# Moving the gate product to the middle of a pair, and casting k before summing it

## The chip, the cores and the metric

The kernel runs on one core of a Trainium2 chip. The core has a matrix engine (TensorE, "PE" in the profile, with its weight loads as "PEld"), VectorE (DVE), ScalarE (ACT), GpSimd (POOL) and SyncE (SP), which issues most DMAs. Each engine works through its own instruction queue; they meet at semaphores. The metric is the device time of one execution in microseconds (us). The runs of the kernel before took 334.65, 334.62 and 332.92 us.

## The reference

A block-sparse causal attention (4 batches, 8 heads, 768 positions, head size 64) is followed by a Fourier mix and a feed-forward layer. The part of the attention around the change, shortened:

```python
k_rep = k.reshape(B, H, 12, 64, D).mean(axis=3)          # one mean per block of 64 keys
gate_scores = np.einsum('bhsd,bhnd->bhsn', q, k_rep)
gate_scores = np.where(causal, gate_scores, -1e9)
top_idx = np.argsort(gate_scores, axis=-1)[..., -3:]     # the three best blocks, and the own block
scores = np.matmul(q, k.transpose(0, 1, 3, 2)) / np.sqrt(D)
scores = np.where(mask_of(top_idx, own_block) & (pos[:, None] >= pos[None, :]), scores, -1e9)
attn = softmax(scores)
attn_out = np.matmul(attn, v)
...
X = np.real(np.fft.fft(np.fft.fft(x, axis=1), axis=2))    # x: attn_out as (4, 768, 512)
u = x + X
un = (u - mean(u)) / np.sqrt(var(u) + 1e-6)
out = u + np.maximum(un @ w_ch1, 0.0) @ w_ch2             # 512 -> 2048 -> 512
```

## The kernel before

Two heads of a batch make a pair, and there are 16 pairs (`kk` from 0 to 15, four to a batch). Each pair goes through these stages, which are functions in the code:

- `stage_AA(kk, who)` calls `stage_A` for two halves. With `who=1` it transposes k: three matmuls (L279) put half of the positions into a PSUM tile `tp`. From this tile VectorE sums k over blocks (`kr12`, L292), and the tile is also cast to 16 bits into `kI` in two pieces, one for each head `e` (L311 on ScalarE; below pair 7 one of the four pieces of a pair is cast by VectorE, L309). After the second half the sums are copied into the operand of the gate product (`kr24`, L297; from pair 8 on split into two 16-bit parts `krx`, L304 and L305). With `who=0` it transposes q, copies it from PSUM (L285, from pair 8 on L287 and L288), and GpSimd copies it on into `qg` (L240).
- `stage_B` is the gate product: ten fp32 matmuls with q and the block sums (L323; ten 16-bit ones from pair 8 on, L331). VectorE adds the causal term (`gsb`, L325), finds the eight largest values ten times (`mx`, L340) and writes the mask `gmp` (L342, L346 or L348).
- `stage_C` transposes the mask on PE (`gt`, L354), and VectorE copies it into rows 64 to 75 of `qg` for either head (L357). The scores then contain the mask, since `kI` holds large negative numbers in the same rows.
- `stage_S` is one sixth of the scores: step `p` of a pair is third `p % 3` of head `p // 3`. Matmuls (L386, and L390 for the diagonal below pair 7) fill one of two PSUM tiles `sc`, and ScalarE's exponential (L391) empties it into `ptl`. So a step's matmuls wait for the exponential two steps earlier.
- `stage_AV(kk, e)` multiplies by v (21 matmuls, L412); VectorE normalises (`rcp` L417, `x` L418). Head 1 of a pair also runs `fold`, additions for the Fourier step, mostly on GpSimd.

All PSUM tiles but `sc` share a pool of four buffers. PE and GpSimd run in the order in which the code emits their work (`tc.manual_schedule`). For VectorE, ScalarE and the DMA queues a scheduler chooses the order, work that is emitted earlier having priority when it is ready.

The main loop (L729 to L766) emits, for each pair, six steps. Every step emits `stage_S`, then some filler, then the other stages that a table assigns to the step, then filler again. Before the change the steps of a usual pair `kk` hold: step 0 the k transposes of pair `kk + 2` (A1); step 1 the output of pair `kk - 1`, head 1 (AV1); step 2 the q transposes of pair `kk + 2` (A0), the v cast on GpSimd, and the issue of the q and k loads of pair `kk + 4` on SP; step 3 the gate transposes of pair `kk + 1` (C); step 4 the output of this pair's head 0 (AV0); step 5 the gate product of pair `kk + 2` (B). The v loads of pair `kk + 2` are issued in step 0. Pair 6 (`NORM_SLOT`) has another table, since the normalisation of batch 0 falls into it; its missing gate product, that of pair 8, runs in step 1 of pair 7. A prologue prepares pairs 0 and 1 up to their gate products, with `stage_W` matmuls on constants in between.

Filler is the Fourier mix and the feed-forward work: `stage_S1` and `stage_S2` (Fourier, L480 to L521), `stage_N` (normalisation), `stage_T` (transposes, L562), `stage_M1` (L578) and `stage_M2` (L592). `filler` pulls as much as a running credit allows, counted by half steps. Units of the chain S1, S2, T become due by a planned clock `feed.now`, to which every emitted stage adds a planned cost and which advances by at least `PACE` for each step; gaps such as `s1_gap` keep a unit from being emitted before its inputs can be there.

Of the kernel before, what the change touches and what calls it, by code (L numbers as in the profile page):

```python
# [118 lines left out]
def kernel(  # L119
# [9 lines left out]
    nc = tc.nc  # L129
    B, H, S, D = q.shape  # L130
# [133 lines left out]
    def stage_A(kk, who, g):  # L264
        d = P[kk]
        src = d["qn"] if who == 0 else d["kn"]
        if who == 0 and g == 0:
            d["qt"] = apool.tile([128, S], FP, tag="qT32", name=f"qT32_{kk}")
            if kk >= SPLIT:
                parts = d["qt"].bitcast(F16)  # L270
                d["qh"], d["ql"] = parts[:, 0:S], parts[:, S:2 * S]
            d["qg"] = [qg_t[e][kk % 3] for e in range(2)]
        if who == 1 and g == 0:
            d["kI"] = [kI_t[e][kk % 3] for e in range(2)]
            d["kr12"] = spool.tile([128, NB], FP, tag="kr12", name=f"kr12_{kk}", bufs=2)
            d["kr24"] = kr24_t[kk % 2]
        ps = pst([128, 3, 128], f"tp_{kk}_{who}_{g}")
        for i in range(3):
            nc.tensor.transpose(ps[:, i, :],  # L279
                                src[:, 3 * g + i, :, :].rearrange("p h d -> p (h d)"), id32)  # L280
        flat = ps.rearrange("p a c -> p (a c)")
        cols = slice(384 * g, 384 * (g + 1))
        if who == 0:
            if kk < SPLIT:
                (nc.scalar.copy if kk == LATE else nc.vector.tensor_copy)(out=d["qt"][:, cols], in_=flat)  # L285
            else:
                nc.scalar.activation(out=d["qh"][:, cols], in_=flat, func=AF.Copy, scale=QS)  # L287
                STT(out=d["ql"][:, cols], in0=flat, scalar=QS, in1=d["qh"][:, cols], op0=MULT, op1=SUB)  # L288
            if g == 1 and kk != LATE:
                cast_q(kk)  # L290
        else:
            nc.vector.tensor_reduce(out=d["kr12"][:, 6 * g:6 * g + 6],  # L292
                                    in_=ps.rearrange("p a (x c) -> p a x c", x=2),
                                    axis=mybir.AxisListType.X, op=ADD)
            if g == 1 and kk < SPLIT:
                for e in range(2):
                    nc.vector.tensor_copy(out=d["kr24"][64 * e:64 * e + 64, NB * e:NB * (e + 1)],  # L297
                                          in_=d["kr12"][64 * e:64 * e + 64, :])
            elif g == 1:
                d["krx"] = krx_t[kk % 2]  # L300
                for e in range(2):
                    r, c = slice(64 * e, 64 * e + 64), slice(NB * e, NB * (e + 1))
                    hi, lo = d["krx"][r, 0, c], d["krx"][r, 1, c]
                    nc.vector.tensor_scalar(out=hi, in0=d["kr12"][r, :], scalar1=QS, scalar2=None, op0=MULT)  # L304
                    STT(out=lo, in0=d["kr12"][r, :], scalar=QS, in1=hi, op0=MULT, op1=SUB)  # L305
            for e in range(2):
                dst, src_ = d["kI"][e][0:64, cols], flat[64 * e:64 * e + 64]
                if kk < EARLY and g == 1 and e == 1:
                    nc.vector.tensor_copy(out=dst, in_=src_)  # L309
                else:  # L310
                    nc.scalar.copy(out=dst, in_=src_)  # L311


    NG = NST - 1
# [287 lines left out]
    def queue_batch(b, start):  # L602
        last = start
        units = []

        s1_gap = 6.0 if b else 3.5
        s2_gap = 1.8 if 0 < b < B - 1 else 1.0
        t_gap = {0: 4.0, B - 1: 6.0}.get(b, 7.5)
        for dt in (1, 0):
            last = Unit(lambda dt=dt: stage_S1(b, dt), S1_COST, last, s1_gap if dt == 1 else 0.0)  # L610
            units.append(last)
        for kt in range(NST):
            last = Unit(lambda kt=kt: stage_S2(b, kt), S2_COST, last, 2.5 if kt == 0 else s2_gap)
            units.append(last)
        for st in range(NST):
            last = Unit(lambda st=st: stage_T(b, st), T_COST, last, t_gap if st == 0 else 0.2,
                        allowed=(lambda: b == 0 or m1_left[b - 1] == 0))
            units.append(last)

        def arm():  # L620
            def m1(it):
                stage_M1(b, it)
                m1_left[b] -= 1
            for it in range(NIT):
                feed.bulk.append(Unit(lambda it=it: m1(it), M1_COST))
# [11 lines left out]
    def filler(kk, half):  # L637


        i = 12 * kk + half  # L640
        key = 12 * (3 * NP) + 32
        if i < key:
            work, left = 2 * BATCH + 3 * CHAIN, key - i
        else:
            work, left = 2 * BATCH + 3 * CHAIN + (NIT - 4) * M1_COST, 12 * NK - i
        state["credit"] = min(state["credit"], 1.0) + (work - state["spent"] - state["credit"]) / left
        done = feed.pull(state["credit"])
        state["credit"] -= done
        state["spent"] += done

    def main(fn, cost, *a):
        fn(*a)
        feed.spend(cost)
# [2 lines left out]
        stage_A(kk, who, 0)  # L656
        stage_A(kk, who, 1)

    PACE = 1.4
    with tc.manual_schedule(engines={mybir.EngineType.PE, mybir.EngineType.Pool}):  # L660
        nc.vector.memset(warm, 0.0)
        nc.scalar.dma_start(id32, dr["ident32"].ap())
# [46 lines left out]
        def after_av(kk):  # L709
            b, hp = divmod(kk, NP)  # L710
            if hp == NP - 1:
                u = Unit(lambda: None, 0.0)
                u.done(feed.now)
                queue_batch(b, u)

        @contextmanager
        def behind_norm(kk):

            if kk != NORM_SLOT:
                yield  # L720
                return
            with tc.issue_after(X[0]["normed"].ins):
                yield

        USUAL = dict(A1=0, AV1=1, A0=2, C=3, AV0=4, B=5)
        NORM = dict(A1=4, AV1=1, A0=5, C=3, AV0=4, B=6)
        for kk in range(NK):  # L729
            at = NORM if kk == NORM_SLOT else USUAL  # L730
            for p in range(6):
                t_in = feed.now
                main(stage_S, 0.39, kk, p // 3, p % 3)
                filler(kk, 2 * p)
                if p == 0 and kk + 2 < NK:
                    load_v(kk + 2)
                if p == at["AV1"] and kk > 0:
                    with behind_norm(kk):
                        main(stage_AV, 0.65, kk - 1, 1)
                    after_av(kk - 1)  # L740
                if p == 1 and kk - 1 == NORM_SLOT:
                    main(stage_B, 0.35, kk + 1)
                if p == at["A1"] and kk + 2 < NK:
                    main(stage_AA, 0.7, kk + 2, 1)
                if p == at["C"] and kk + 1 < NK:
                    main(stage_C, 0.3, kk + 1)
                if p == at["AV0"]:
                    main(stage_AV, 0.65, kk, 0)
                    if kk + 2 == LATE:
                        pool_after(ft[3][:, 0, 2:3])  # L750
                        cast_q(kk + 2)
                        cast_v(kk + 2)
                if p == at["A0"]:
                    if kk + 2 < NK:
                        main(stage_AA, 0.7, kk + 2, 0)
                        if kk + 2 != LATE:
                            cast_v(kk + 2)
                    if kk == 0:
                        stage_W(4)
                    if kk + 4 < NK:  # L760
                        load_qk(kk + 4)
                if p == at["B"] and kk + 2 < NK:
                    main(stage_B, 1.05 if kk + 2 < SPLIT else 0.35, kk + 2)
                filler(kk, 2 * p + 1)
                if feed.now < t_in + PACE:
                    feed.now = t_in + PACE  # L766
            if kk == 1:
                load_fft()
            if kk in (2, 4):
                pool_after(P[kk + 2]["qt"])  # L770
                load_w1(kk // 2 - 1)
            if kk in (6, 7):
                pool_after(P[kk + 2]["qt" if kk + 2 < SPLIT else "ql"])
                load_w2(2 * kk - 12)
                load_w2(2 * kk - 11)
# [35 lines left out]
```

## Time and profile before

| what | us |
|---|---|
| runs: median (lowest to highest) | 334.62 (332.92 to 334.65) |
| profiled execution, device time | 332.94 |
| its span, first to last instruction | 331.2 |
| first score matmul of pairs 0, 1, 2, 3, 4, 5, 6 | 16.66, 24.85, 32.88, 40.84, 48.73, 62.22, 73.43 |
| first feed-forward matmul (L578) | 86.95 |
| last exponential of the attention starts | 249.3 |

A row of a timeline gives start, length, engine, line, operation, tiles and count; a bracket at its end says how long the engine sat idle before it, and what ended that. Equal instructions in a row are merged into one line. In the chain of waits the lengths are those by which the end was held up, not the durations. The busy time of PE includes the pipeline's latency: matmuls of 512 columns overlap and follow each other at 0.216 us where nothing stops them (96 in 20.73 us near the end), while the row of their group says 379 ns for one.

Between pair 0 and the first feed-forward matmul there is little filler, and a pair takes about 8 us. Later a step carries about 2 us of filler, and a pair takes 18 to 20 us.

### The profile page before, as it was taken

The numbers are of one execution on the slowest core, as the hardware profiler recorded it, in microseconds if no ns is written. First come the engines' busy times: TensorE is split into PE (matmuls) and PEld (weight loads), VectorE is DVE, ScalarE is ACT, GpSimd is POOL, SyncE is SP. The second block draws the span as 40 slices with busy tenths as digits, with TensorE's granted clock in tenths as the row PEclk, the third lists the DMA queues.
The fourth block names the chain that finished last, engine by engine and source line by source line (L and its number), as shares of the span: only waits on it lengthen the run. The fifth ranks groups of instructions, "written<-read, shape, count | busy, mean of one in ns | idle before, by whom it ended". The sixth has DMA issues, their size and how long they took to land.

```text
span 331.2 us, 7008 instructions
## 1 busy us (share of the span) xinstructions
PE 311.9 (94%) x2712; PEld 202.9 (61%) x2712; DVE 235.7 (71%) x750; ACT 180.3 (54%) x276; POOL 84.7 (26%) x137
## 2 busy tenths in 40 slices
PE   8799998997889989998999989999999999999995
PEld 3567776876656666555666666656666654556442
DVE  3778889689776898999765898998457588433211
ACT  3188889789965855428486754535764302244000
POOL 8545573352481120504032030502030000000000
PEclk9999999998999999999999999999999999999999
DMA  8997999990799242425324000010000011100021
GB/s 203 230 256 186 246 136 226 155 221 7 165 188 181 54 96 75 103 70 136 99 48 97 2 0 35 32 65 32 34 2 0 2 64 63 65 1 2 32 95 63
DMA packets 85312, 31.18 MB, mean 94 GB/s; under 512 B 77736, under 2 KB 81136, under 8 KB 85280
## 3 DMA queue, kind: packets, MB, share of 16 engines
q1 hardware_dynamic: 79984, 25.88, 31.4%
q0 software_dynamic: 3552, 4.40, 8.5%
q10 hardware_dynamic: 1744, 0.46, 0.6%
q8 instruction: 21, 0.34, 0.4%
q14 instruction: 11, 0.09, 0.1%
HBM read 28.63 MB, written 6.29 MB: 105 GB/s over the span
## 4 chain that ended last, share of the span: by engine, by line
PE 73%; DVE 16%; ACT 7%; issue 1%; POOL 1%; DVEq 0%; ACTq 0%
PE ch L592 22%; PE ha L578 14%; PE sc L386 8%; PE hb L578 7%; PE av L412 5%; ACT kI L311 4%; PE g L323 3%; PE za L480 2%; DVE mx L340 2%; DVE ptl L397 2%; ACT ptl L391 2%; PE tp L279 2%; PE warm L365 2%; PE gt L354 2%; PE mx L507 2%; PE mx L508 2%
## 5 line engine op out<-in xcount | busy, mean ns | idle before, releaser
L391 ACT ACTIVATE ptl<-sc 128x896 f16<-128x896 f32 x96 | 87.3, 919 | 45.9 <-PE sc L386 36.6
L592 PE MATMUL ch<-w_sb,hT 128*128 128x512 f16 x384 | 91.4, 379 | 0.5 <-DVE qT L288 0.5
L578 PEld LDWEIGHTS <-w_sb 128*128 128x128 f16 x512 | 48.8, 97 | 38.6 <-issue 4.7
L578 PE MATMUL ha<-unT,w_sb 128*128 128x512 f16 x256 | 65.7, 378 | 1.8 <-DVE hT L583 1.4
L386 PE MATMUL sc<-qg,kI 76*128 76x512 f16 (+3 forms) x256 | 54.8, 306 | 3.6 <-ACT ptl L391 3.6
L592 PEld LDWEIGHTS <-hT 128*128 128x128 f16 x384 | 36.2, 97 | 35.1 <-issue 0.6
L581 ACT ACTIVATE hT<-ha 128x512 f16<-128x512 f32 x64 | 38.1, 597 | 33.5 <-PE ha L578 33.4
L583 DVE TENSOR_SCALAR hT<-hb 128x256 f16<-128x256 f32 x64 | 26.8, 421 | 28.9 <-PE hb L578 28.7
L578 PE MATMUL hb<-unT,w_sb 128*128 128x256 f16 x256 | 38.4, 272 | 1.1 <-ACT hT L581 0.7
L429 POOL TENSOR_TENSOR fs<-x 128x384 f16<-128x384 f16 x12 | 10.9, 909 | 105.5 <-DVE x L418 91.8
L386 PEld LDWEIGHTS <-kI 76*128 76x128 f16 x256 | 24.0, 100 | 20.3 <-issue 2.8
L311 ACT CAST kI<-tp 64x384 f16<-64x384 f32 x57 | 27.1, 475 | 14.6 <-DVE kr L292 13.6
L595 DVE TENSOR_TENSOR u<-ch,u 128x512 f32<-128x512 f32 x24 | 16.5, 685 | 19.9 <-PE ch L592 19.6
L412 PE MATMUL av<-v,ptl 128*128 128x65 f16 x672 | 26.2, 195 | 0.0
L412 PEld LDWEIGHTS <-ptl 128*128 128x128 f16 x672 | 24.8, 98 | 2.0
L292 DVE TENSOR_REDUCE kr<-tp 128x6 f32<-128x384 f32 x32 | 17.2, 551 | 7.0 <-PE tp L279 7.0
L397 DVE TENSOR_TENSOR ptl<-ptl,ut 128x384 f16<-128x384 f16 x36 | 16.0, 479 | 6.1 <-ACT ptl L391 5.7
L553 ACT ACTIVATE x<-u,nmr,rstd 128x512 f16<-128x512 f32 x12 | 8.9, 806 | 17.7 <-DVE nmr L546 17.6
L418 DVE TENSOR_TENSOR x<-av,rcp 128x384 f16<-128x384 f32 x32 | 17.8, 557 | 0.9
L390 PE MATMUL sc<-ltri,id 128*128 128x128 f16 x84 | 18.4, 219 | 0.0
L240 POOL COPY qg<-qT 64x768 f16<-64x768 f16 x16 | 14.4, 902 | 12.1 <-ACT qT L287 11.6
L520 DVE BATCH_NORM_STATS2 bst<-u 128x6 f32<-128x512 f32 x24 | 16.6, 692 | 1.2 <-ACT u L516 0.7
(112 smaller groups left out, 422.9 us busy)
## 6 DMA issues: line engine op xcount, KB each, us to landing
vn<-in_v_dram SPq DMA_DIRECT2D x32, 192.0 KB, 3.3
out_dram<-u SPq DMA_DIRECT2D x24, 256.0 KB, 2.0
kn<-in_k_dram SPq DMA_DIRECT2D x30, 192.0 KB, 3.3
qn<-in_q_dram SPq DMA_DIRECT2D x30, 192.0 KB, 3.4
w_sb<-in_moe_w_ch_dram POOLq DMA_DIRECT2D x8, 256.0 KB, 7.0
w_sb<-in_moe_w_ch_dram POOLq DMA_DIRECT2D x4, 512.0 KB, 9.5
cs_sb<-c_CS SPq DMA_DIRECT2D x1, 289.5 KB, 4.9
ss_sb<-c_SS SPq DMA_DIRECT2D x1, 289.5 KB, 5.2
```

The costliest lines, as they stand in the source:

```text
L292: nc.vector.tensor_reduce(out=d["kr12"][:, 6 * g:6 * g + 6], in_=ps.rearrange("p a (x c) -> p a x c", x=2), axis=mybir.AxisListType.X, op=ADD)
L311: nc.scalar.copy(out=dst, in_=src_)
L386: nc.tensor.matmul(sp[:, co:co + (a1 - a0)], d["kI"][e][0:76, 128 * jt:128 * (jt + 1)], d["qg"][e][0:76, a0:a1], start=True, stop=not diag)
L390: nc.tensor.matmul(sp[:, co:co + 128], id16, ltri, start=False, stop=True)
L391: nc.scalar.activation(out=pt[:, SEC * s:SEC * (s + 1)], in_=sp[:, 0:SEC], func=AF.Exp, scale=0.125 if kk < SPLIT else 0.125 / QS)
L397: nc.vector.tensor_tensor(out=dg, in0=dg, in1=um, op=MULT)
L412: nc.tensor.matmul(av[:, st, 0:65], pt[:, o:o + 128], d["v16"][:, e, jt, 0:65], start=(cnt == 0), stop=(cnt == 20))
L418: nc.vector.tensor_tensor(out=x_b[:, :, 64 * h:64 * h + 64], in0=av[:, :, 0:64], in1=rcp.to_broadcast([128, NST, 64]), op=MULT)
L578: nc.tensor.matmul(hp_, w1_sb[:, dt, 128 * it:128 * (it + 1)], unT[:, dt, c0:c1], start=(dt == 0), stop=(dt == NDT - 1))
L581: nc.scalar.activation(out=hT[:, c0:c1], in_=hp_, func=AF.Relu)
L583: nc.vector.tensor_scalar(out=hT[:, c0:c1], in0=hp_, scalar1=0.0, scalar2=None, op0=mybir.AluOpType.max)
L592: nc.tensor.matmul(cps, x["hT"][it][:, 128 * st:128 * (st + 1)], w2_sb[:, it, :], start=(it == 0), stop=(it == NIT - 1))
```

## The change

Three things change, and the amount of work is the same before and after.

First, k. From pair 2 on a half of k is cast before it is summed, and the casts and the sum of the second half are not emitted with its transposes, but by `finish_k`, after the scores of the next step. So they stand behind that step's exponential.

Second, the table of steps. A usual pair `kk` now has in step 0 A1 of pair `kk + 2`; in step 1 B of pair `kk + 1`; in step 2 AV1 of pair `kk - 1`; in step 3 A0 of pair `kk + 2`, with its casts and loads, and C of pair `kk + 1`; in step 4 AV0; in step 5 nothing. A gate product thus runs in the pair directly before the one that uses it, two steps ahead of its transposes. Pair 0 has no gate product. Pair 4 keeps AV1 in step 1, has B in step 2, A0 in step 3 and C ahead of AV0 in step 4. Pair 5 has a second gate product, that of pair 7, in step 5.

Third, the planner: `PACE` goes from 1.4 to 1.3, and some gaps of the chain become shorter.

```diff
-            nc.vector.tensor_reduce(out=d["kr12"][:, 6 * g:6 * g + 6],
-                                    in_=ps.rearrange("p a (x c) -> p a x c", x=2),
-                                    axis=mybir.AxisListType.X, op=ADD)
...
+            if kk < 2:
+                sums_k(kk, g, ps)
+                cast_k(kk, g, ps)
+            elif g == 0:
+                cast_k(kk, g, ps)
+                sums_k(kk, g, ps)
+            else:
+                d["tp_k"] = ps
+
+    def finish_k(kk):
+
+        ps = P[kk].pop("tp_k", None)
+        if ps is not None:
+            cast_k(kk, 1, ps)
+            sums_k(kk, 1, ps)
+
+    def cast_k(kk, g, ps):
+        d = P[kk]
+        flat = ps.rearrange("p a c -> p (a c)")
+        cols = slice(384 * g, 384 * (g + 1))
+        for e in range(2):
+            dst, src_ = d["kI"][e][0:64, cols], flat[64 * e:64 * e + 64]
+            if kk < EARLY and g == 1 and e == 1:
+                nc.vector.tensor_copy(out=dst, in_=src_)
+            else:
+                nc.scalar.copy(out=dst, in_=src_)
+
+    def sums_k(kk, g, ps):
...
-        s1_gap = 6.0 if b else 3.5
-        s2_gap = 1.8 if 0 < b < B - 1 else 1.0
-        t_gap = {0: 4.0, B - 1: 6.0}.get(b, 7.5)
+        s1_gap = 6.0 if b else 3.2
+        s2_gap = 1.8 if 0 < b < B - 1 else 1.0 if b else 0.8
+        t_gap = {0: 3.4, B - 1: 6.0}.get(b, 7.0)
...
-            last = Unit(lambda kt=kt: stage_S2(b, kt), S2_COST, last, 2.5 if kt == 0 else s2_gap)
+            last = Unit(lambda kt=kt: stage_S2(b, kt), S2_COST, last, (2.5 if b else 2.2) if kt == 0 else s2_gap)
...
-    PACE = 1.4
+    PACE = 1.3
...
-        USUAL = dict(A1=0, AV1=1, A0=2, C=3, AV0=4, B=5)
-        NORM = dict(A1=4, AV1=1, A0=5, C=3, AV0=4, B=6)
+        USUAL = ["A1", "B", "AV1", "A0 C", "AV0", ""]
+        LAYOUT = {
+            0: ["A1", "", "", "A0 W C", "AV0", ""],
+
+            NP: ["A1", "AV1", "B", "A0", "C AV0", ""],
+            NORM_SLOT - 1: ["A1", "B", "AV1", "A0 C", "AV0", "B+"],
+
+            NORM_SLOT: ["", "AV1", "", "C", "A1 AV0", "A0"],
+        }
         for kk in range(NK):
-            at = NORM if kk == NORM_SLOT else USUAL
             for p in range(6):
                 t_in = feed.now
                 main(stage_S, 0.39, kk, p // 3, p % 3)
+                if kk + 2 < NK:
+                    finish_k(kk + 2)
                 filler(kk, 2 * p)
                 if p == 0 and kk + 2 < NK:
                     load_v(kk + 2)
...
+                for what in LAYOUT.get(kk, USUAL)[p].split():
...
+                    n = kk + (2 if what == "B+" else 1)
+                    if what in ("B", "B+") and n < NK:
+                        main(stage_B, 1.05 if n < SPLIT else 0.35, n)
                 filler(kk, 2 * p + 1)
```

`sums_k` holds the sum and the copies or splits that follow it, as they stood in `stage_A` before (L292 to L305).

More of the change, by code (lines that the diff above doesn't have):

```diff
@@ L291, in stage_A @@
         else:
-            nc.vector.tensor_reduce(out=d["kr12"][:, 6 * g:6 * g + 6],
-                                    in_=ps.rearrange("p a (x c) -> p a x c", x=2),
-                                    axis=mybir.AxisListType.X, op=ADD)
[L295 to L305, printed above, removed]
@@ L306, in stage_A @@
-            for e in range(2):
[L307 to L311, printed above, removed]
+            if kk < 2:
[6 more added lines that the diff above has]
+                d["tp_k"] = ps
@@ new lines, in sums_k @@
+    def sums_k(kk, g, ps):
+        d = P[kk]
+        nc.vector.tensor_reduce(out=d["kr12"][:, 6 * g:6 * g + 6],
+                                in_=ps.rearrange("p a (x c) -> p a x c", x=2),
+                                axis=mybir.AxisListType.X, op=ADD)
+        if g == 1 and kk < SPLIT:
+            for e in range(2):
+                nc.vector.tensor_copy(out=d["kr24"][64 * e:64 * e + 64, NB * e:NB * (e + 1)],
+                                      in_=d["kr12"][64 * e:64 * e + 64, :])
+        elif g == 1:
+            d["krx"] = krx_t[kk % 2]
+            for e in range(2):
+                r, c = slice(64 * e, 64 * e + 64), slice(NB * e, NB * (e + 1))
+                hi, lo = d["krx"][r, 0, c], d["krx"][r, 1, c]
+                nc.vector.tensor_scalar(out=hi, in0=d["kr12"][r, :], scalar1=QS, scalar2=None, op0=MULT)
+                STT(out=lo, in0=d["kr12"][r, :], scalar=QS, in1=hi, op0=MULT, op1=SUB)
@@ L736 @@
                     load_v(kk + 2)
[L737 to L754, printed above, removed]
+                for what in LAYOUT.get(kk, USUAL)[p].split():
+                    if what == "AV1" and kk > 0:
+                        with behind_norm(kk):
+                            main(stage_AV, 0.65, kk - 1, 1)
+                        after_av(kk - 1)
+                    if what == "AV0":
+                        main(stage_AV, 0.65, kk, 0)
+                        if kk + 2 == LATE:
+                            pool_after(ft[3][:, 0, 2:3])
+                            cast_q(kk + 2)
+                            cast_v(kk + 2)
+                    if what == "A1" and kk + 2 < NK:
+                        main(stage_AA, 0.7, kk + 2, 1)
+                    if what == "A0" and kk + 2 < NK:
                         main(stage_AA, 0.7, kk + 2, 0)
@@ L757 @@
                             cast_v(kk + 2)
-                    if kk == 0:
+                        if kk + 4 < NK:
+                            load_qk(kk + 4)
+                    if what == "W":
                         stage_W(4)
[L760 to L763, printed above, removed]
+                    if what == "C" and kk + 1 < NK:
+                        main(stage_C, 0.3, kk + 1)
+                    n = kk + (2 if what == "B+" else 1)
+                    if what in ("B", "B+") and n < NK:
+                        main(stage_B, 1.05 if n < SPLIT else 0.35, n)
                 filler(kk, 2 * p + 1)
```

## The prediction

> **What bounds the kernel now.** I began with busy shares, then cut the span into attention pairs, then followed the chain of waits through one pair, and last read what one engine does in it. All sums are made against the profiled execution: 332.94 us, of which 331.2 us are span.
>
> ```profile
> PE 311.9 (94%) x2712; PEld 202.9 (61%) x2712; DVE 235.7 (71%) x750; ACT 180.3 (54%) x276; POOL 84.7 (26%) x137
> ```
>
> ```profile
> 24.85:32.88 8.03, 7.34 (x99) 6.01 (x99) 6.65 (x26) 6.71 (x10) 4.16 (x5) 1.00 0.75 181
> 32.88:40.84 7.96, 7.34 (x99) 6.01 (x99) 6.65 (x26) 6.71 (x10) 4.12 (x6) 1.00 1.05 256
> ```
>
> The first block is the page's shares, the second a table by stretch (columns: length, then busy PE, PEld, DVE, ACT, POOL, then clock, DMA, GB/s). I cut at the first score matmul of pairs 1, 2 and 3; pair 0 begins at 16.66. PE's 94% is an average over two stages. From 87 us to the end PE carries the feed-forward work and its waits, summed, are only 5.1 us up to 285 us; nothing that the change does to attention can win more than that there. Before 87 us no engine is full: a pair takes 8 us while PE, ACT and DVE are each busy for 6.7 to 7.3. A loop of waits sets that pace:
>
> ```profile
> 31.96 1.10 PE g L323 x10
> ...
> 33.40 0.82 DVE mx L340 x10
> 34.22 0.47 DVE kr L292
> ...
> 34.71 0.47 ACT kI L311
> ...
> 36.17 0.82 ACT ptl L391
> ...
> 37.13 0.38 PE sc L386
> ```
>
> The chain of waits (start, length, what): the gate product ends, VectorE takes its maxima, then sums k, then ScalarE casts k three times (34.71 to 36.17), then comes an exponential, and only then has the next score matmul a free buffer. A cast begins 0.02 us after the sum that it follows: the two readers of one transposed tile take turns. Now the same stretch on VectorE:
>
> ```profile
> 33.08 0.28 DVE L325 TENSOR_TENSOR gsb<-g,cz 128x120 f32<-128x120 f32 x1 [0.80 <-PE g L323]
> 33.40 0.82 DVE L340 MAX8 mx<-gsb 128x8 f32<-128x12 f32 x10
> 34.13 0.55 DVE L292 TENSOR_REDUCE kr<-tp 128x6 f32<-128x384 f32 x1
> 34.59 0.28 DVE L342 TENSOR_TENSOR gmp<-gsb,mx 128x120 f16<-128x120 f32 x1
> 34.77 0.56 DVE L292 TENSOR_REDUCE kr<-tp 128x6 f32<-128x384 f32 x1
> 35.24 0.22 DVE L346 TENSOR_TENSOR gmp<-gmp,oth 128x120 f16<-128x120 f16 x1
> 35.37 0.35 DVE L297 COPY kr<-kr 64x12 f32<-64x12 f32 x2
> 35.75 0.20 DVE L417 RECIPROCAL rcp<-av 128x6 f32<-128x6 f32 x1
> ...
> 36.57 0.56 DVE L309 CAST kI<-tp 64x384 f16<-64x384 f32 x1
> 37.16 1.02 DVE L285 COPY qT<-tp 128x384 f32<-128x384 f32 x2
> 38.21 1.00 DVE L357 COPY qg<-gt 12x640 f16<-12x640 f16 x2
> 39.46 0.20 DVE L417 RECIPROCAL rcp<-av 128x6 f32<-128x6 f32 x1 [0.25 <-PE av L412]
> ```
>
> Start to start, its prices are: gsb 0.32, ten maxima 0.78 (with the next op's overlap), a k sum 0.46, the two mask steps 0.19 and 0.13, kr copies 0.38, an output normalisation (rcp, x) 0.82, k cast 0.59, two q copies 1.05, two gate copies (qg) 1.00, the first of them 0.50. With a second k sum and a second normalisation that is 7.0 of 7.96; the rest is its two waits, 0.80 and 0.25. The gate copies follow right on their transposes (38.18) and end at 39.2, while the next pair's scores start at 40.84: 1.6 us to spare.
>
> **Part 1: cast first, sum second.** It takes from ScalarE the wait for the sum: 0.15 us at 34.71, and 0.44, 0.27, 0.00 and 0.74 in pairs 0, 1, 3 and 4, 0.3 on average. It is no term of its own, for by what follows ScalarE no longer sets a pair's length. After 87 us such waits exist too (6.7 us in 4), but PE is full there, so I count nothing. The price goes to VectorE: a sum now follows two casts, 0.97 us later, and the second half waits for the next exponential, 0.92 us, too. The second tile keeps its PSUM buffer longer, by one score step. Nobody needs the sum soon, as its gate product now runs a pair later.
>
> **Part 2: the gate product moves.** Nothing is added in total: 10 matmuls (1.08 us of PE in the pairs below 8, 0.26 in the later ones) and 1.42 us of VectorE per pair change place. PE's floor for a pair, from the timeline, is six scores at 0.505, two outputs at 0.64, two sets of transposes at 0.66, gate product 1.08, gate transposes 0.39: 7.1 us. ACT's is six exponentials at 0.915 and three casts at 0.487: 6.95. The middle of a pair is where ScalarE has casts to do, so the even spread should let the pair fall from 7.96 towards 7.1 to 7.4, if nothing else binds.
>
> I think VectorE binds. Count from a pair's first score matmul. Its exponential begins 0.76 later (40.84 to 41.60) and takes 0.92, two casts 0.97: the first k sum can start at 2.65. The gate product ends at 0.505 + 0.66 + 0.505 + 1.08 = 2.75. So VectorE, having finished the last pair's remnants (second gate copy 0.50, normalisation 0.82) at 1.3, stands idle to 2.65. From there until the first gate copy it has the first sum 0.46, gate chain 1.42, k cast 0.59, second sum 0.46, kr 0.38, normalisation 0.82, q copies 1.05 and the copy itself 0.50: 5.68. All of these but the last are issued earlier in the program and are ready before the gate transposes are: the k cast at about 4.1, in the middle of the maxima, so that it, the sum and the kr copies push the mask to some 5.9, while PE reaches the gate transposes at 2.75 + 0.505 + 0.64 + 0.505 + 0.66 = 5.06 and waits 0.8 to 1.0. Then 2.65 + 5.68 + 0.1 = 8.4, when the next pair's scores may start, for they read the copied rows. Queued behind PE's wait are the output of this head and two scores, hence two exponentials. The bounds: 7.8 if the k cast (0.59) slips behind the gate copies, 8.7 if VectorE also waits for ScalarE (0.26 us before a k cast at 44.16 is such a wait). I take 8.4, +0.44 for each of pairs 1 to 3: **+1.3** (-0.4 to 2.2).
>
> **Pair 0** drops its gate product (the prologue made it), but its transposes of q and the warm matmuls (0.9 us), until now run during a wait, move behind the fourth score. First exponential to 18.28 as now, two casts to 19.25, second exponential to 20.17; 0.14 later the fourth score may start, 20.3; then q transposes, warm matmuls, gate transposes (1.95 together), fourth and fifth score to 23.3; the fifth's exponential, which frees the buffer that the next pair's first score takes, ends about 24.4. So 24.55 for 24.85: **-0.3**.
>
> **Pairs 4 and 5.** Pair 4 has 0.77 and 0.46 us of PE waiting for ScalarE, which hide its gate product (1.08; open, it would cost that). The gate transposes, 0.39, now fall behind the first Fourier step, into a stretch in which PE never stops (55.5 to 76.4): **+0.4**. Pair 5 gets two gate products in place of one, the one taken from pair 4's end, and statistics of 0.87 per Fourier step in the same VectorE queue: **+0.3** (0 to 1).
>
> **Everything else moved.** Output e=1 and the q transposes go one step later, with two POOL copies, the v cast and four k/q loads on SP's queue. POOL is busy 4.1 of 7.96; loads land 3.3 us after issue and are read over a pair later; the next v load is a pair's start away. The weight loads that POOL holds behind q move by the same step and are needed at 87 us. Cost nothing; without that slack, one step, 1.3 us, once. Adding up the planner's new costs, gaps and pace, batch 0's Fourier, transpose and feed-forward steps fall into the same score steps as before (pair 4 step 4, pair 6 step 3, pair 7 step 0), later batches' within one or two, and the order after pair 15 is identical. **0**.
>
> **The dense stage.**
>
> ```profile
> PE ha L578 <- DVE hT L583: 1.4, 2, 0.7
> ...
> PE gt L354 <- DVE hT L583: 1.1, 1, 1.1
> ```
>
> These waits of PE between 87 and 285 us are for PSUM buffers: four serve all but the scores. Now q and gate transposes stand together (three buffers at once) and a k tile keeps one longer. Nine pairs, from a gain of 2 (less than half of the 5.1 us of waits) to a loss of 2.5 (0.28 a pair); I take **+0.4**.
>
> Sum: 1.3 - 0.3 + 0.4 + 0.3 + 0.4 = **+2.1**, so 335.0 against 332.94.
>
> One row can add a step to it:
>
> ```profile
> 80.00:81.00 1.00, 1.00 (x7) 0.95 (x6) 0.95 (x3) 1.00 (x3) 0.99 (x2) 0.50 0.00 0
> ```
>
> In this stretch the granted clock is 0.50, and about 0.9 or less from 79 to 84 us: which makes some 3.4 us at half clock, 1.7 us lost, after PE had waited 0.15 and 1.56 us at 76 to 78. Waits of 0.77 and 0.46 at 53 us led to no such drop. My 1.0 at the gate transposes plus 0.3 before the next pair lies between.
>
> The Trainium skill ("TensorE: Matmul & The Clock Gate", Part 1 on the HAM clock gate) says that the clock halves after an idle window of about 3.4 us. By that page no wait named here would be long enough and the sum would stay as it is; the row shows a drop after less, so I let the row decide and keep 1.7 in the upper end.
>
> **Rivals.** *The even spread works* (33%): VectorE's queue puts the gate copies early enough and pairs run at 7.3. Three pairs at -0.66, pair 0 at -0.3: -2.3, 330.6; with the drop at 80 us gone too, 328.9. For it: three floors near 7; against it: the idle stretch counted above. *Nothing to measure* (14%): pairs come out at 8.0 and what is left is swallowed by the normalisation wait at 76 us (1.56): 332.9. *PSUM buffers run out in the dense stage* (8%), slower: decided if a k tile is still held when the second feed-forward unit asks; price by the 0.66 to 0.69 us that one such wait costs, in nine pairs, 6 us: 339. Against it: PE waits at only 9 places there now. My forecast has 45%, its own range 333.3 to 337.5 (pairs at 7.8 to 8.7; one drop less, or one more, in part).
>
> **How the numbers follow.** The runs shown are 332.92, 334.62 and 334.65; with the profiled one, two lie at each of two levels 1.7 us apart, which is about what one half-clock stretch costs. The median is the upper level. I put the time half a step (0.84) above the sum: 335.8. The range takes in the even spread, 330.6 and lower by some tenths, and above the drop and part of the buffer case, on either level: 330.0 to 338.8. About 0.5% can be told from no change. Slower by more: three quarters of the forecast, the buffer case, some of the rest, 0.44; faster: four fifths of the even spread and a little, 0.28; between, 0.28.
>
> **What would show it.** Right: score starts of pairs 1 to 4 some 8.4 apart; PE waiting before the gate transposes (L354's row) for the mask; gate copies on VectorE directly ahead of a pair's first score; k casts no longer behind sums. Wrong: pairs at 7.1 to 7.4 with ScalarE without gaps, gate copies done a microsecond before they are read; or early pairs as I say and the change made up after 87 us.

## The result, and the profile after

| | before | after |
|---|---|---|
| runs: median (lowest to highest), us | 334.63 (332.92 to 334.92) | 342.35 (342.16 to 342.53) |
| profiled execution, us | 332.94 | 342.53 |
| its span, us | 331.2 | 340.8 |
| first score matmul of pairs 0 to 6, us | 16.66, 24.85, 32.88, 40.84, 48.73, 62.22, 73.43 | 16.94, 26.71, 35.30, 43.83, 52.38, 67.20, 80.63 |
| first feed-forward matmul, us | 86.95 | 93.45 |

The kernel became slower: ratio 1.0241, interval 1.0207 to 1.0276. The forecast was 335.8, its range ended at 338.8. In the profiled executions the loss of 9.6 us of span divides into 0.3 ahead of pair 0, 1.6 in pair 0, 1.8 in pairs 1 to 3, 1.3 in pair 4, 2.2 in pair 5, a gain of 0.7 in pair 6, and 3.1 from the first feed-forward matmul to the end. In some executions the whole run is slower at a lower granted clock (one of `sums_first` below took 387.79 us): medians are over all executions, ratios leave such ones out.

In the changed kernel the lines have moved: the sums of k are L322, its casts L318 (ScalarE) and L316 (VectorE), the gate product L347, the mask L366 and L370, its transposes L378, the gate copies L381, the scores L410, the exponential L415, the feed-forward matmuls L602 and L616. The table by stretch for pair 1 (same columns as before):

```profile
26.71:35.30 8.59, 7.33 (x100) 5.98 (x99) 5.87 (x25) 6.36 (x9) 1.09 (x2) 1.00 0.54 119
```

No engine is busy for longer than before in this pair, and it takes 0.6 us longer. The timeline of VectorE shows why (start, length, operation; the bracket is idle time and what ended it):

```profile
29.66 0.28 DVE L349 TENSOR_TENSOR gsb<-g,cz 128x120 f32<-128x120 f32 x1 [2.53 <-PE g L347]
29.97 0.17 DVE L364 MAX8 mx<-gsb 128x8 f32<-128x12 f32 x1
30.06 0.54 DVE L322 TENSOR_REDUCE kr<-tp 128x6 f32<-128x384 f32 x1
30.52 0.74 DVE L364 MAX8 mx<-gsb 128x8 f32<-128x12 f32 x9
31.29 0.56 DVE L316 CAST kI<-tp 64x384 f16<-64x384 f32 x1
31.86 0.56 DVE L322 TENSOR_REDUCE kr<-tp 128x6 f32<-128x384 f32 x1
32.34 0.28 DVE L366 TENSOR_TENSOR gmp<-gsb,mx 128x120 f16<-128x120 f32 x1
32.53 0.34 DVE L327 COPY kr<-kr 64x12 f32<-64x12 f32 x2
32.90 0.22 DVE L370 TENSOR_TENSOR gmp<-gmp,oth 128x120 f16<-128x120 f16 x1
```

```profile
33.18 0.46 PE L378 MATMUL gt<-id,gmp 128*44 128x128 f16 x5 [1.25 <-DVE gmp L370]
```

VectorE stands idle for 2.53 us, because the sums, which it could do now, stand behind ScalarE's casts and these behind exponentials. Then everything comes at once: two sums, a cast and two small copies (2.0 us in all) fall between the gate's sum and its mask, the mask is done 3.46 us after 29.66, and TensorE waits 1.25 us for it. The same waits are in the groups of VectorE's sums (busy time, mean ns, then idle time ahead of them and what ended it). Before:

```profile
L292 DVE TENSOR_REDUCE kr<-tp 128x6 f32<-128x384 f32 x32 | 17.2, 551 | 7.0 <-PE tp L279 7.0
```

After:

```profile
L322 DVE TENSOR_REDUCE kr<-tp 128x6 f32<-128x384 f32 x32 | 17.6, 553 | 18.8 <-ACT kI L318 12.6
```

VectorE never waited for a cast before a sum, and now does so for 12.6 us. Cut at 93.5 us, half of it, 6.3 us in 6 waits, lies in the dense stage. There TensorE has work while VectorE waits, and the price comes later. One such case, first on VectorE, then on TensorE:

```profile
193.42 0.56 DVE L322 TENSOR_REDUCE kr<-tp 128x6 f32<-128x384 f32 x1 [1.80 <-ACT kI L318]
193.89 0.41 DVE L607 TENSOR_SCALAR hT<-hb 128x256 f16<-128x256 f32 x1
194.91 0.56 DVE L322 TENSOR_REDUCE kr<-tp 128x6 f32<-128x384 f32 x1 [0.60 <-ACT kI L318]
...
203.20 1.17 DVE L459 TENSOR_TENSOR fo<-ft,ft 128x762 f16<-128x762 f16 x1
204.29 1.17 DVE L459 TENSOR_TENSOR fc<-ft,ft 128x762 f16<-128x762 f16 x1
205.39 1.01 DVE L288 SCALAR_TENSOR_TENSOR qT<-tp,qT 128x384 f16<-128x384 f32 x2
```

```profile
183.94 0.61 PE L602 MATMUL hb<-unT,w_sb 128*128 128x256 f16 x4 [1.62 <-DVE qT L288]
...
205.99 1.02 PE L616 MATMUL ch<-w_sb,hT 128*128 128x512 f16 x4 [1.25 <-DVE qT L288]
```

Two sums wait for casts, and so do the evictions `hT` and the Fourier additions (L459) queued behind them on VectorE, though these have nothing to do with k. From 194.91 on VectorE has no gap, and TensorE pays some 10 us later: its wait at 205.99 is 1.25 us, and 0.22 at the same place in `layout_only`, the kernel with the new table and the old order of k (see below). Not every long wait here comes from k: the one of 1.62 us at 183.94 is 1.22 in `layout_only`, and one of 1.06 at 125.76 is 1.02, so these belong mostly to the new table.

Pair 0 lost by another wait, TensorE's timeline and the table by stretch (the third number from the end is the granted clock):

```profile
20.86 0.38 PE L410 MATMUL sc<-qg,kI 76*128 76x512 f16 x1 [1.59 <-ACT ptl L415]
...
22.56 1.91 PE L389 MATMUL warm<-warm 128*128 128x512 f16 x4
```

```profile
22.00:23.00 1.00, 1.00 (x6) 0.66 (x5) 0.76 (x2) 0.47 (x1) 0.00 (x0) 0.50 1.00 227
```

Three casts stand ahead of the second exponential, so the fourth score starts at 20.86, not at 20.3 as forecast; the clock then falls to half from about 21.4 to 24.8 us, and the four filling matmuls take 1.91 us instead of 1.02. The half clock is what costs most here, and it doesn't always come: in the profiled `mask_first` and `sums_behind_mask` (below) the same wait is 1.59 us too, the clock stays at 1.00, and pair 0 takes 8.38 us between first exponentials, against 10.01 here and 8.19 before the change. (Their totals are no lower, 341.63 and 341.93 us; their pair 0 begins 0.9 and 1.1 us later.)

### The profile page after: what moved, and what is told of

It reads as the page before. It is cut to its first block, busy times and chain, and to the rows that moved or that the text cites. A ratio compares the mean times of both kernels' runs of the same rounds, so it can differ in the third digit from the quotient of the medians.

```text
span 340.8 us, 7014 instructions
## 1 busy us (share of the span) xinstructions
PE 314.1 (92%) x2712; PEld 204.0 (60%) x2712; DVE 233.2 (68%) x750; ACT 178.9 (52%) x276; POOL 83.5 (24%) x137
## 4 chain that ended last, share of the span: by engine, by line
PE 63%; DVE 24%; ACT 7%; issue 2%; DMA 1%; POOL 1%; ACTq 0%; DVEq 0%
PE ch L616 20%; PE ha L602 11%; PE sc L410 6%; PE hb L602 6%; PE av L436 4%; DVE kr L322 3%; ACT kI L318 3%; ACT ptl L415 3%; DVE mx L364 3%; PE tp L279 3%; PE g L347 2%; PE za L504 2%; DVE ft L459 2%; DVE hT L607 2%; PE unt L586 1%
## 5 line engine op out<-in xcount | busy, mean ns | idle before, releaser
L415 ACT ACTIVATE ptl<-sc 128x896 f16<-128x896 f32 x96 | 86.6, 917 | 55.5 <-PE sc L410 37.4
L616 PE MATMUL ch<-w_sb,hT 128*128 128x512 f16 x384 | 91.5, 379 | 3.0 <-DVE qT L288 1.3
L602 PEld LDWEIGHTS <-w_sb 128*128 128x128 f16 x512 | 48.8, 97 | 38.9 <-issue 2.7
L602 PE MATMUL ha<-unT,w_sb 128*128 128x512 f16 x256 | 65.7, 378 | 1.7 <-ACT hT L605 0.8
L616 PEld LDWEIGHTS <-hT 128*128 128x128 f16 x384 | 36.4, 97 | 38.0 <-issue 3.4
L410 PE MATMUL sc<-qg,kI 76*128 76x512 f16 (+3 forms) x256 | 54.3, 306 | 1.8 <-ACT ptl L415 1.7
L602 PE MATMUL hb<-unT,w_sb 128*128 128x256 f16 x256 | 38.4, 273 | 1.7 <-DVE qT L288 1.6
L410 PEld LDWEIGHTS <-kI 76*128 76x128 f16 x256 | 23.9, 99 | 18.2 <-issue 2.2
L318 ACT CAST kI<-tp 64x384 f16<-64x384 f32 x57 | 26.9, 472 | 7.6 <-DVE kr L322 4.9
L322 DVE TENSOR_REDUCE kr<-tp 128x6 f32<-128x384 f32 x32 | 17.6, 553 | 18.8 <-ACT kI L318 12.6
L381 DVE COPY qg<-gt 12x640 f16<-12x640 f16 x32 | 15.5, 483 | 3.1 <-PE gt L378 2.3
```

The lines of the kernel that those rows point to most:

```text
L322: nc.vector.tensor_reduce(out=d["kr12"][:, 6 * g:6 * g + 6], in_=ps.rearrange("p a (x c) -> p a x c", x=2), axis=mybir.AxisListType.X, op=ADD)
L410: nc.tensor.matmul(sp[:, co:co + (a1 - a0)], d["kI"][e][0:76, 128 * jt:128 * (jt + 1)], d["qg"][e][0:76, a0:a1], start=True, stop=not diag)
L415: nc.scalar.activation(out=pt[:, SEC * s:SEC * (s + 1)], in_=sp[:, 0:SEC], func=AF.Exp, scale=0.125 if kk < SPLIT else 0.125 / QS)
L602: nc.tensor.matmul(hp_, w1_sb[:, dt, 128 * it:128 * (it + 1)], unT[:, dt, c0:c1], start=(dt == 0), stop=(dt == NDT - 1))
L616: nc.tensor.matmul(cps, x["hT"][it][:, 128 * st:128 * (st + 1)], w2_sb[:, it, :], start=(it == 0), stop=(it == NIT - 1))
```

## The experiments

All ratios are to the kernel before, run beside it on the same chip. "K part" means casts before sums, with the second half behind the next step's scores.

**The three parts alone.** `k_only`: the kernel before with the K part. `layout_only`: the changed kernel with the old order of k.

```diff
-            if kk < 2:
-                sums_k(kk, g, ps)
-                cast_k(kk, g, ps)
...
-            else:
-                d["tp_k"] = ps
+            sums_k(kk, g, ps)
+            cast_k(kk, g, ps)
```

`planner_only`: the kernel before with the new `PACE` and gaps. `dense_old`: the changed kernel, from pair 7 on with the old table.

```diff
+        DENSE = ["A1", "AV1", "A0", "C", "AV0", "B+"]
...
```

> The kernel before with the k part alone: casts first, sums second, second half behind the next step's exponential; step table and planner as before. Theory (the new step table makes the loss, since it puts the mask, the q copies and the gate copies close together in VectorE's queue): the gate product still has four steps until its mask is read, so nothing is late; pairs 1 to 3 stay at 7.8 to 8.0 us, the time within 1 us of the kernel before. Rival (the late sums and the longer held PSUM tile make the loss): pairs 1 to 3 at 8.3 or more, PE waits after 87 us for PSUM buffers, time 3 us or more above.

> The changed kernel with the old k order: sum, then casts, all emitted with the transposes; the new step table and planner stay. Theory (the step table makes the loss): pairs 1 to 3 at 8.2 to 8.7 us and the time at 340 to 343. Rival (the k part makes it): pairs at 7.9 or less, the time at 336 or less. If both are needed, it lies between.

> The kernel before with PACE 1.3 and the shorter gaps alone. Theory: the same units fall into nearly the same steps, so the time stays within 1 us of the kernel before. Rival (units come due too early and PE waits for them): 2 us or more above, with new waits of PE at the Fourier steps or the transposes of the normalised rows.

> The changed kernel, but from pair 7 on with the old step table (AV1 in step 1, q transposes in step 2, gate transposes in step 3, gate product of the pair after next in step 5); the k part stays everywhere. Theory (after 87 us the loss comes from AV1, q transposes and gate transposes standing next to each other, so that q copies wait behind the additions of fold and PSUM buffers stay full): the 3 us that the changed kernel loses between the first feed-forward matmul and the end go to 0 to 1, the time is 339 to 340. Rival (the k tile that is held a step longer uses up the buffers): no change, 342.

Measured: k_only 342.61 us, ratio 1.0267 (1.0224 to 1.031); layout_only 335.35, 1.0052 (1.0028 to 1.0075); planner_only 333.81, 1.0012 (0.9993 to 1.003); dense_old 347.58, 1.0423 (1.0359 to 1.0486). Three of four expectations missed. My theory, that the table makes the loss and the K part is harmless, fell: the K part alone costs as much as the whole change. Yet its early pairs are the shortest of these four runs, 7.4 us; its loss lies in the dense stage (so does that of `dense_old`, which has the old table there: pairs 7 to 14 take 158.35 and 158.68 us, 149.42 before). VectorE's timeline before and in `k_only`, then TensorE's in `k_only`:

```profile
108.49 1.01 DVE L292 TENSOR_REDUCE kr<-tp 128x6 f32<-128x384 f32 x2
```

```profile
110.65 0.56 DVE L322 TENSOR_REDUCE kr<-tp 128x6 f32<-128x384 f32 x1 [0.89 <-ACT kI L318]
111.64 0.56 DVE L322 TENSOR_REDUCE kr<-tp 128x6 f32<-128x384 f32 x1 [0.43 <-PE sc L410]
```

```profile
120.65 1.44 PE L602 MATMUL ha<-unT,w_sb 128*128 128x512 f16 x3 [2.05 <-DVE hT L607]
```

From the second sum to this matmul VectorE has no gap; the matmul waited 0.66 us at the same place in the kernel before.

**Where the K part costs.** `k_early` is k_only with the old order from pair 8 on; `old_k_dense` is the changed kernel with the same edit; `k_at_once` is k_only without the deferral (casts, then sums, both at once); `sums_behind_mask` is the changed kernel with `finish_k` moved behind the step's other stages.

```diff
-            if kk < 2:
+            if kk < 2 or kk >= SPLIT:
                 sums_k(kk, g, ps)
                 cast_k(kk, g, ps)
```

> The kernel before (its own step table), with the k part of the change for k of pairs 2 to 7 alone; k of pairs 8 to 15 is summed and cast at once as before. Theory 1 (the early pairs gain 0.5 us each from the casts ahead of the sums, and all of the 8.8 us that the k part lost with this table was lost behind 87 us, by k tiles of the second batch that are held across a step): scores of pairs 1 to 3 start 7.4 us apart, pairs 7 to 12 last what they last before, total 330.5 to 332.5, ratio 0.99 to 1.0. Theory 2 (the early gain itself is paid back later, since it shifts the feed-forward units against the pairs): the dense part loses several us again, total 336 to 342.

> The kernel before with the k part's order alone: casts first and sums second for both halves, but the second half at once, not behind the next step's scores. Theory 1 (the deferral is what costs: it keeps one PSUM tile a step longer): the dense part lasts what it lasts before, total 330 to 334. Theory 2 (the order is what costs: ScalarE's casts come ahead of VectorE's sum, so both engines have the k tile later or VectorE is reordered): 340 to 344 as with the whole k part.

> The changed kernel with the second half of k cast and summed behind all work of the next step, that is behind the next pair's gate product and its mask chain on VectorE, instead of ahead of it. Theory (in the early pairs the late sums and the cast of k stand in VectorE's order between the gate's maxima and its mask and make the gate transposes wait 1.25 us): that wait goes, pairs 1 to 3 fall from 8.55 to 7.8 or less; the k tile is held longer still, so the dense part loses as much as now or more (3 to 9 us against before); total 338 to 345. Rival (the wait has nothing to do with the k sums, the mask chain is late in itself): pairs 1 to 3 stay at 8.5.

> The changed kernel with k of pairs 8 to 15 summed and cast at once as before; step table and everything else as changed. Theory 1 (the 3.1 us that the changed kernel loses behind 87 us come from the k part, of the second batch's pairs): total 339 to 340, dense part as long as before within 1 us, early part as in the changed kernel (+6.5). Theory 2 (they come from the step table, or from the shift of the feed-forward units against the pairs that the longer early part brings): total 341.5 to 343.

Measured: k_early 332.38, ratio 0.9959 (0.9928 to 0.9989); k_at_once 336.4, 1.0081 (1.0045 to 1.0118); sums_behind_mask 341.93, 1.0238 (1.0198 to 1.0277); old_k_dense 339.76, 1.0176 (1.0135 to 1.0216). So k_early beats the kernel before by 0.4%, and with the old table the whole loss lies with k of pairs 8 to 15; with the new table some 2 us do. k_at_once came out between its two theories: order and deferral both cost. sums_behind_mask tells little: VectorE's order is not that of emission, the sums stayed ahead of the mask, and pairs 1 to 3 stayed at 8.5 to 8.7 us.

**A held PSUM tile, or a VectorE that waits?** Deferred work keeps one of four PSUM buffers a step longer, and makes VectorE wait for ScalarE. `hold_only` adds to the kernel before a read of one element at the later place, for pairs 8 to 15, and leaves the code of sums and casts as it is. `sums_at_once` is the changed kernel, `sums_at_once_old_table` is k_only, both with the sums of pairs 8 to 15 ahead of the casts while the second half's casts stay late. `mask_first` gives the mask chain of pairs 2 to 7 priority on VectorE.

```diff
...
+            nc.vector.tensor_copy(out=late_read, in_=ps[0:1, 0, 0:1])
...
```

```diff
+        with tc.high_priority() if 1 < kk < SPLIT else nullcontext():
...
```

> The changed kernel with the mask chain of the gate (maxima, comparison, product) put ahead of other ready work in VectorE's order for pairs 2 to 7; one sum and the cast of k still fall into the gaps between its steps, the second sum and the copies of k's sums come behind it. Theory (the chain from the gate's sum to the mask takes 3.46 us because 2.0 us of k work stands in it, against 2.7 in the kernel with the new step table and the old k order): the chain falls to about 2.6 us, TensorE's wait ahead of the gate transposes from 1.25 to 0.4 us or less, pairs 1 to 3 from 8.55 to 7.7 to 7.9 us, total 339 to 341. Rival (the mask is late because the gate product itself starts late, behind the half clock of pair 0): the pairs stay at 8.5, total 342 to 343.

> The kernel before, with one read of a single element added for pairs 8 to 15: it keeps the PSUM tile of k's second half until after the next step's scores, as the change does, while sums and casts stay where they are. Theory H (the deferral costs because a tile is held a step longer and the next tiles have to wait for a buffer): the dense part loses some 5 us, total 337 to 340. Theory V (it costs because the sums now stand behind ScalarE's casts, so that VectorE waits with everything that is queued behind them): no loss, total 333 to 334.5.

> The changed kernel, with k of pairs 8 to 15 summed at once and ahead of its casts; the casts of its second half stay behind the next step's scores. Theory V (VectorE waiting at the sums for ScalarE's casts, 6.3 us behind 93 us where it waited for nothing before, is what the dense part loses): that wait is gone and the total comes to 339.5 to 340.5, as with the whole old order there (339.76). Theory H (the held tile): it stays at 341.5 to 343.

> The kernel before with the k part in pairs 2 to 7, and in pairs 8 to 15 the sums at once and ahead of the casts, with the casts of the second half behind the next step's scores. Theory V: as fast as with the old order in pairs 8 to 15, 331.5 to 333. Theory H (held tile): the dense part loses 4 us or more, total 336 or more.

Measured: mask_first 341.63, ratio 1.0254 (1.021 to 1.0298); hold_only 335.18, 1.0054 (1.0031 to 1.0078); sums_at_once 340.41, 1.0218 (1.018 to 1.0256); sums_at_once_old_table 332.52, 0.9978 (0.9956 to 1.0001). With the old table a held tile with late casts costs nothing that can be told from k_early, and late sums cost 9 us: VectorE's waiting is the cause there. With the new table the interval of sums_at_once overlaps that of the changed kernel; its profiled pairs 7 to 14 take 147.97 us, 2.0 less than in the changed kernel and near the 147.61 of old_k_dense. A held tile may cost something: hold_only lost 1.8 us (0.0054 of 333.2), but its profile shows only 0.5 in pairs 7 to 14 (149.94 us for 149.42) and 0.6 of waits of TensorE for the added read, so where the rest goes is open.

mask_first missed. VectorE's timeline has the mask ready 2.5 us after the gate's sum, as wanted:

```profile
28.96 0.28 DVE L349 TENSOR_TENSOR gsb<-g,cz 128x120 f32<-128x120 f32 x1 [2.53 <-PE g L347]
...
31.26 0.21 DVE L371 TENSOR_TENSOR gmp<-gmp,oth 128x120 f16<-128x120 f16 x1
31.50 0.56 DVE L322 TENSOR_REDUCE kr<-tp 128x6 f32<-128x384 f32 x1
```

but the gate transposes on TensorE wait on:

```profile
32.11 0.46 PE L379 MATMUL gt<-id,gmp 128*44 128x128 f16 x5 [0.88 <-DVE kr L322]
```

They don't read the sum. What they share with it is the pool of PSUM buffers: the sum is the last reader of k's tile and ends at 32.06, 0.05 us before they start. The other three buffers then hold the two halves of q and an output, which VectorE goes on reading until 33.0 us or later. So I read this as a wait for that buffer. In the early pairs late sums then hurt twice, and pulling the mask ahead of them only changes which of the two is last.

**The sums back to the front, all else as changed.** `sums_first` sums at once and ahead of the casts in all pairs; the casts stay late, the table and the planner as changed. `w_early` is the changed kernel with pair 0's filling matmuls one step earlier, ahead of the scores that wait. `sums_first_w_early` has both.

```diff
-            elif g == 0:
-                cast_k(kk, g, ps)
-                sums_k(kk, g, ps)
-            else:
+            elif g == 0:
+                sums_k(kk, g, ps)
+                cast_k(kk, g, ps)
+            else:
+                sums_k(kk, g, ps)
                 d["tp_k"] = ps
...
             cast_k(kk, 1, ps)
-            sums_k(kk, 1, ps)
...
-            0: ["A1", "", "", "A0 W C", "AV0", ""],
+            0: ["A1", "", "W", "A0 C", "AV0", ""],
```

> The changed kernel with pair 0's four filling matmuls in step 2, ahead of the scores that wait 1.59 us for an exponential, instead of in step 3 behind them. Theory (TensorE stands idle 1.59 us there, its clock is then granted at half from 21.4 to 24.6 us, and the filling matmuls themselves run at half clock, 1.91 instead of 1.02 us): the wait falls to about 0.6, the clock stays full, pair 0 falls from 9.77 to 8.0 to 8.4 us, total 340.5 to 341.2. Rival (pair 0 is set by its exponentials and mask, and what is saved is waited for at the gate transposes): pair 0 stays above 9.3, total 342 to 343.

> The changed kernel with k summed at once and ahead of its casts in all pairs; the casts of the second half stay behind the next step's scores. Theory (the early pairs lose because the two sums leave the time in which VectorE waits for the gate product anyway, 2.5 us, and enter the chain of the mask, while the held tile only matters after that): the chain falls from 3.46 to 2.7 us, pairs 1 to 3 from 8.55 to 7.8 to 7.9, the dense part as in the kernel with the old order there; total 335.5 to 337.5. Rival (the held tile: the gate transposes wait for its buffer until the late casts are done): pairs 1 to 3 at 8.2 or more, total 338.5 or more.

> Both of the above in one. If the two losses are separate, the gains add: total 333.7 to 336, some 7 us below the changed kernel, and within 0.6% of the kernel before. If pair 0's wait returns in another place, 336 to 338.

Measured: w_early 341.77, ratio 1.0232 (1.0162 to 1.0302); sums_first 334.32, 1.0013 (0.9978 to 1.0048); sums_first_w_early 332.91, 1.0004 (0.9964 to 1.0044). Moving the sums alone takes the loss away, more than I expected (335.5 to 337.5). VectorE's timeline of sums_first:

```profile
26.48 1.02 DVE L322 TENSOR_REDUCE kr<-tp 128x6 f32<-128x384 f32 x2 [0.62 <-PE tp L279]
27.54 0.35 DVE L327 COPY kr<-kr 64x12 f32<-64x12 f32 x2
28.40 0.28 DVE L349 TENSOR_TENSOR gsb<-g,cz 128x120 f32<-128x120 f32 x1 [0.51 <-PE g L347]
...
30.47 0.21 DVE L370 TENSOR_TENSOR gmp<-gmp,oth 128x120 f16<-128x120 f16 x1
```

The sums fill the time in which VectorE waited for the gate product, they start 1.03 us after the pair's first score matmul (25.45) instead of 3.35 (26.71 to 30.06), and the gate transposes follow at 30.74 with no wait. Pairs 1 to 3 are then 0.5 us shorter each than before the change; pairs 4 and 5, longer by 0.7 and 0.4, take most of that back. Pair 0 has no half clock in this execution. w_early missed: pair 0 fell by 2.5 us (by the 8.38 us above, some 1.6 of it is the half clock, which is not there), but the next pair's gate transposes waited instead, and the clock fell to half there (TensorE's timeline, table by stretch):

```profile
31.07 0.46 PE L378 MATMUL gt<-id,gmp 128*44 128x128 f16 x5 [1.65 <-DVE gmp L370]
```

```profile
33.00:35.00 2.00, 2.00 (x11) 1.37 (x10) 0.75 (x2) 1.08 (x3) 1.88 (x3) 0.50 1.06 334
```

With the sums in front that wait is gone. The median with both edits is 1.4 us below that of sums_first, but the two ratios differ by 0.0009 only and their intervals overlap: no gain of w_early is shown.

Where the spans of single profiled executions divide, cut at the first exponential of a pair:

| us | before | after | layout_only | k_only | k_early | sums_first |
|---|---|---|---|---|---|---|
| to pair 0's first exponential | 17.36 | 17.64 | 17.91 | 18.32 | 17.23 | 18.25 |
| pair 0 | 8.19 | 10.01 | 10.53 | 7.69 | 7.68 | 8.14 |
| pairs 1 to 3 | 23.94 | 25.71 | 23.42 | 22.23 | 22.23 | 22.43 |
| pair 4 | 13.49 | 15.23 | 14.19 | 13.56 | 13.56 | 14.19 |
| pair 5 | 11.21 | 12.79 | 11.62 | 11.76 | 11.76 | 11.62 |
| pair 6 | 12.17 | 11.77 | 11.80 | 12.16 | 12.17 | 11.77 |
| pairs 7 to 14 | 149.42 | 150.00 | 147.62 | 158.35 | 149.40 | 147.97 |
| rest | 95.4 | 97.6 | 97.6 | 95.4 | 95.4 | 97.6 |
| span | 331.2 | 340.8 | 334.7 | 339.4 | 329.4 | 332.0 |

The new table moves some 2 us from pairs 7 to 14 into the rest, whatever k does: compare these rows among kernels with one table. The two long pairs 0, after and layout_only, are those with a half-clock stretch in them (21.4 to 24.8 and 21.7 to 25.1 us), whatever the order of k.

## Why the prediction was wrong

The direction was right, the size wrong, and it was mainly one step that failed: part 1, "It is no term of its own", with its reasons "Nobody needs the sum soon" and, for the dense stage, "PE is full there, so I count nothing". It is true that nobody needs the sum soon. But what is queued behind a sum on VectorE waits with it (at 193.42 above), and its PSUM tile is held. With the sums put back and nothing else changed, 7.6 us go (0.0228, the difference of the ratios 1.0241 and 1.0013, of 334). The sum of the prediction was +2.1 us and the profiled spans differ by 9.6; of these 7.5 us, 4.6 are what the K part adds in pairs 4 and 5 (2.2) and 7 to 14 (2.4), by the columns after and layout_only, where the prediction gave the late sums no price. Some 1.6 more are the half clock in pair 0, which is chance as far as the runs show.

- **Pairs 1 to 3: +1.3 forecast, +1.8 measured.** Right in mechanism and nearly in size: starts 8.53 to 8.59 us apart for 8.4, TensorE waiting 1.25 us for the mask for 0.8 to 1.0. The count of VectorE's queue held because it had the late sums in it. I didn't draw the conclusion that the sums made this loss, and that with them in front the pairs would be at 7.5, the "even spread" that I gave 33%.
- **Pair 0: -0.3 forecast, +1.6 measured.** I let two casts go ahead of the second exponential; it was three, and the fourth score came 0.6 us later than forecast. But the loss is the half clock, which I had kept in the upper end only: without it the late sums leave pair 0 at 8.38 us, 0.2 above the kernel before. Nor is it the order of k that brings it, for layout_only, with the sums in front, has it too and takes 10.53 us. In pair 6, where I took 1.7 us as its price, it cost nothing: the pair takes 12.17 us with it (before) and without it (k_early).
- **Pairs 4 and 5: +0.4 and +0.3 forecast, +1.3 and +2.2 measured.** Part of pair 5's is the moved gate product (1.08 of TensorE), which I had counted as covered. With the sums in front pair 4 falls by 1.0 and pair 5 by 1.2 us.
- **Dense stage: +0.4 forecast (-2 to +2.5), +3.1 measured,** of which 2.4 belong to the K part (150.00 less 147.62 in pairs 7 to 14). The reason that I gave for the upper end, a held buffer, is at most the smaller part: hold_only puts it at 1.8 us (1.0 to 2.6 by its interval) with the old table, where the K part costs 9, and sums_at_once_old_table at nothing. The larger one is VectorE waiting. With the new table the K part costs only about a quarter of the 9; why, no run shows.
- **Planner: 0, confirmed** (1.0012, interval from 0.9993).
- **Rival "PSUM buffers run out in the dense stage"** (8%, 339) had the sign and, in the early pairs of mask_first, even the mechanism. Its total was too low, for it left out the VectorE queue.

By ratios the parts are: table and planner alone +1.7 us, K part in pairs 2 to 7 alone -1.4, both together +5.9 (old_k_dense), all of it +8.0. So 5.6 us are an interaction in the early pairs (5.9 - 1.7 + 1.4), and some 2 the K part in the later ones. The profiled pairs 1 to 5, which have no half clock, give the same 5.6: 53.7 us in old_k_dense, 49.2 in layout_only, 47.5 in k_early, 48.6 before. Neither part alone would have shown the first: under the old table the gate product comes at a pair's end, and late sums fall behind its mask; the new one puts it in the middle, just where the late sums arrive.

Open is how the 9 us of k_only's dense stage divide between the order (pairs 7 to 14 take 149.42 us before, 153.32 in k_at_once) and the deferral (158.35): the runs show that both go with the sums, not why they have these sizes. Part of either is the clock: in k_only it stands at half from 119.7 to 126.5 us, where TensorE works again from 120.65, in k_at_once from 118.1 to 121.6. Half of the working time, some 2.9 and 1.4 us, is my estimate of what that costs. For the early pairs under the new table no run separates order from deferral.

## What to carry to other kernels

When two engines read one buffer in turns, put first the reader whose engine is idle then, not the one whose result is wanted first: the second one's wait is paid by all that is queued behind it. Before an operation is called free because its result has slack, ask what stands behind it on its engine, and which buffer it keeps. And test parts of a change in pairs, not only alone: here two parts of +1.7 and -1.4 us made +5.9.

## What the runs showed of the hardware

The granted clock fell to half for about 3.4 us at a time (in k_only for 6.8) close to waits of TensorE, and the length of the wait doesn't decide whether it does. The wait of 1.59 us in pair 0 had a half-clock stretch behind it in the changed kernel (wait until 20.9 us), and none in mask_first (21.8) and sums_behind_mask (22.0). The wait of 1.56 us for the normalisation had one in the kernel before (78.2), and none in k_early (76.5). The waits of 0.77 and 0.46 us in pair 4 passed without one in the kernel before, and in planner_only half clock followed from 55.1 us on. So waits far below the 3.4 us that the Trainium skill names ("TensorE: Matmul & The Clock Gate", Part 1) can be enough; where page and runs differ, the runs decide. That page says that the monitor's window runs freely, which would fit; no run here shows it. Nor does half clock always cost time: some 1.6 us in pair 0, nothing in pair 6.

VectorE's operations with two inputs in SBUF slow down beside GpSimd: in k_only two additions of the Fourier step (128x762) take 0.55 us each, and the next two of the same shape 1.18 each, beside GpSimd's copies of q (116.76 to 118.68 us); in the kernel before two mask products take 1.87 us beside such copies, where their group's mean in the changed kernel is 0.352. This agrees with what the Trainium skill says of a port pair that one of the two engines holds for a whole instruction ("SBUF — State Buffer", SBUF: two separate sides). Where a backlog pushes such operations beside GpSimd's copies, as in k_only and at 203.20 in the changed kernel, it grows by 0.6 us for each.
